# Late-converted weights used from the tiles they are converted into, in turns with loaded ones

## The chip, the core and the metric

The kernel runs on one core of a Trainium2 chip. The metric is device time in microseconds (us) of one execution; the median of three runs stands for the kernel. TensorE (PE) multiplies, VectorE (DVE), ScalarE (ACT) and GpSimd (POOL) work on elements, and SyncE (SP) asks for transfers between HBM and the on-chip buffers. In the kernel before all transfers are asked for by SP's queue, which goes through its list in order.

## What is computed

The reference chains three parts over 2304 tokens (4 batches of 576), cut here to what matters:

```python
q_p, k_p = phi(q), phi(k)                  # linear attention, 4 batches x 8 heads
x = (q_p @ (k_p.T @ v)) / (q_p @ sum(k_p)) # -> x: 2304 x 512
h = x @ w_in                               # first layer, 512 -> 2048
x = (h * cos(h)) @ w_out                   # second, 2048 -> 512
P = sinkhorn(x @ w_gate)                   # 8 experts
out = sum(P[:, e:e+1] * (relu(x @ w1[e]) @ w2[e]) for e in range(8))
```

The weights `w_in` and `w_out` arrive as 64-bit numbers, viewed as pairs of 32-bit integers.

## The kernel before

Every fp32 product is made of three products of rounded parts: a number is split into `hi` (fp32r) and `lo = x - hi`, and a product is `hi*hi + hi*lo + lo*hi`. Each weight therefore exists as a pair of tiles.

**Weights of the middle part.** `w_in` and `w_out` are cut into 16 **units** of 128 hidden columns (`NF1`). A unit has two **halves** of 512 KB: half `2f` is the piece of `w_in` of unit f (tile `wi`), half `2f+1` the piece of `w_out` (tile `wo`). So there are 32 halves, 0 to 31. A half is **converted** from its 64-bit form in seven operations, each on 128 x 512 elements:

- `conv_fetch` (L124): SP loads the raw half into `raw64`, of which there are two buffers (the profile calls the source `in_moe_w_dram`);
- `conv_low` (L129): ACT makes `csgn` from the low words;
- `conv_size` and `conv_floor` (L135, L140): DVE makes and clips `cmag`; `conv_high` (L144): DVE shifts `cmag`, and takes the sign into `csgn`;
- `conv_join` (L149): POOL adds `csgn` to `cmag`;
- `conv_round` (L153): ACT copies to the `hi` part; `conv_rest` (L158): POOL subtracts to the `lo` part. Both go into a tile `csp` of a pool of its own;
- `conv_store` (L162): SP stores `csp` to HBM as `wd[f]`. `load_half1` (L96) loads it again later, into `wi` or `wo`, of which there are four buffers each.

**Order of the work.** `attention()` runs 16 head pairs through a software pipeline whose order is the string `ORDER`; one half is converted in each turn, halves 0 to 16 in all. Then the middle part goes over five blocks of tokens: blocks 0 to 2 (512 tokens, one after the other), and blocks 3 and 4 together. For one block `moe1_steps` (L579) walks over the 16 units: `moe1_l1` makes 12 products for unit f into `ph`, the function `h*cos(h)` follows in five operations (ACT `y`, ACT `t`, DVE `y`, ACT `y` (the sine), DVE `h`) and the split of its result in two more (ACT `hh`, DVE `hl`), and `moe1_l2` of unit f, 12 products into `acc`, is issued two units later (`LAG`). Each 6 products are a **step**; a unit is four steps.

The generator `convert()` (L379) converts halves 17 to 31. Each `next(conv)` issues a third of a half's work, and in block 0 one is issued after every step:

```python
for blk in range(B - 1):
    for i, _ in enumerate(moe1_steps(blk)):
        tick()
        if blk == 0:
            next(conv, None)
```

`weights1` (L572) loads the units in the order 0 to 15, each `wi` two units ahead, and pulls more of `conv` where a half that is to be loaded isn't converted. The order of the engines' instructions is written out in this way and kept; where the loads stand in SP's queue is chosen by a scheduler. Block 0 is therefore the only block in which half of the weights are made while they are needed; blocks 1 to 4 load all of them from `wd`. The last part (the experts) follows and is not touched.

In names below, `raw_2989` is the raw half 18, and the next numbers follow half by half; `wd_97` to `wd_112` are the stored units 0 to 15.

Of the kernel before, what the change touches and what calls it, by code (L numbers as in the profile page):

```python
# [9 lines left out]
F32 = mybir.dt.float32  # L10
F32R = mybir.dt.float32r
# [14 lines left out]
def kernel(ctx: ExitStack, tc: tile.TileContext, q, k, qk_rem, v, w_phi,  # L26
                         moe_w, moe2_w_gate, moe2_w1, moe2_w2, out):
    nc = tc.nc
    P = 128
    B, NP, _, MAIN = q.shape  # L30
    D = v.shape[-1]
    NTT, _, DM = out.shape
# [3 lines left out]
    NF1 = moe_w.shape[0]  # L36
# [38 lines left out]
    pe, ve, se, ge = Engine(nc.tensor), Engine(nc.vector), Engine(nc.scalar), Engine(nc.gpsimd)  # L75
# [5 lines left out]
    def pool_lo(lo, raw, hi):  # L81
        ge.tensor_tensor(out=lo, in0=raw, in1=hi.bitcast(F32), op=ALU.subtract)
# [4 lines left out]
    def act_hi(hi, raw):  # L87
        se.copy(out=hi, in_=raw)
# [4 lines left out]
    ps_h = ctx.enter_context(tc.tile_pool(name="ps_h", bufs=1, space=PSUM))  # L93
    wpool = mctx.enter_context(tc.tile_pool(name="wpool", bufs=4, side="right"))

    def load_half1(f, i):  # L96
        w = wpool.tile([P, 2, DM], F32R, name=f"w{'io'[i]}")
        nc.sync.dma_start(out=w.bitcast(F32), in_=wd[f][:, i, :, :])
        parts = [w[:, s, :] for s in range(2)]
        return [x.rearrange("p (k f) -> p k f", k=KC) for x in parts] if i == 0 else parts  # L100

# [11 lines left out]
    vpool = ectx.enter_context(tc.tile_pool(name="vpool", bufs=2))  # L113
    apool = actx.enter_context(tc.tile_pool(name="apool", bufs=2, side="right"))
# [4 lines left out]
    wd = [dpool.tile([P, 2, 2, DM], F32, name=f"wd{f}") for f in range(NF1)]  # L119
# [4 lines left out]
    def conv_fetch(h):  # L124
        raw = vpool.tile([P, DM, 2], I32, name="raw64")
        nc.sync.dma_start(out=raw.rearrange("p f t -> p (f t)"), in_=moe_w32[h // 2, h % 2])
        halves[h] = {"raw": raw}

    def conv_low(h):  # L129
        st = halves[h]  # L130
        st["sgn"] = vpool.tile([P, DM], I32, name="csgn")
        se.activation(out=st["sgn"].bitcast(F32), in_=st["raw"][:, :, 0].bitcast(U32), func=AF.Copy,
                      scale=2.0 ** -51, bias=2.0)

    def conv_size(h):  # L135
        st = halves[h]
        st["mag"] = vpool.tile([P, DM], I32, name="cmag", bufs=3)
        ve.tensor_scalar(out=st["mag"], in0=st["raw"][:, :, 1], scalar1=2 ** 31 - 1, scalar2=None, op0=ALU.bitwise_and)
# [10 lines left out]
    def conv_join(h):  # L149
        st = halves[h]  # L150
        ge.tensor_tensor(out=st["mag"], in0=st["mag"], in1=st["sgn"], op=ALU.add)

    def conv_round(h):  # L153
        st = halves[h]
        st["sp"] = vpool.tile([P, 2, DM], F32R, name="csp")
        act_hi(st["sp"][:, 0, :], st["mag"].bitcast(F32))

    def conv_rest(h):  # L158
        st = halves[h]
        pool_lo(st["sp"][:, 1, :], st["mag"].bitcast(F32), st["sp"][:, 0, :])  # L160

    def conv_store(h):  # L162
        st = halves.pop(h)
        nc.sync.dma_start(out=wd[h // 2][:, h % 2, :, :], in_=st["sp"].bitcast(F32))

    VW = 66
    vx_t = []
# [11 lines left out]
    def load_heads(b, p):  # L179
        st = {"b": b, "p": p}  # L180
        for nm, src in (("k", k), ("q", q)):
            st[nm] = apool.tile([P, MAIN], F32, name=f"T{nm}")
            nc.sync.dma_start(out=st[nm], in_=src[b, p])
        st["r"] = apool.tile([P, P], F32, name="Tr")
        nc.sync.dma_start(out=st["r"], in_=qk_rem[b, p])
        return st
# [13 lines left out]
    first = load_heads(0, 0)  # L200
# [9 lines left out]
    def defer(n, fn):  # L210
        late.append([n, fn])
# [112 lines left out]
    def normalize(st):  # L324
        pn = st["pn"]
        pv = pn.rearrange("p (a c) -> p a c", a=2)[:, :, 0:4 * VW].rearrange("p a (j c) -> p a j c", j=4)
        pz = pn[:, 4 * VW:5 * VW]
        r = apool.tile([P, 9], F32, name="rd", bufs=2)
        rv = r[:, 0:8].rearrange("p (a j) -> p a j", a=2)
        ve.tensor_scalar(out=rv, in0=pv[:, :, :, D], scalar1=1e-6, scalar2=None, op0=ALU.add)  # L330
        ve.tensor_scalar(out=r[:, 8:9], in0=pz[:, D:D + 1], scalar1=1e-6, scalar2=None, op0=ALU.add)
        ve.reciprocal(r, r)
        xn = apool.tile([P, 4, 2, D], F32, name="xn")
        xr = apool.tile([P, D], F32, name="xr")
        ve.tensor_tensor(out=xn.rearrange("p j a d -> p a j d"), in0=pv[:, :, :, 0:D], in1=rv.unsqueeze(3).to_broadcast([P, 2, 4, D]), op=ALU.mult)
        ve.tensor_scalar(out=xr, in0=pz[:, 0:D], scalar1=r[:, 8:9], scalar2=None, op0=ALU.mult)
        st["xn"], st["xr"] = xn, xr
# [41 lines left out]
    def convert():  # L379
        first = B * NP + 1  # L380
        for h in range(first, NHALF + 2):
            if h < NHALF:
                if h not in halves:
                    conv_fetch(h)
                conv_low(h)
                conv_size(h)
                conv_floor(h, ve)
            if h - 2 >= first:
                conv_rest(h - 2)
            yield  # L390
            if h < NHALF:
                conv_high(h)
            if first <= h - 1 < NHALF:
                conv_round(h - 1)
            if h - 2 >= first:
                conv_store(h - 2)
                done_conv[0] = h - 1
            yield
            if h < NHALF:
                conv_join(h)  # L400
            if h + 1 < NHALF and h + 1 not in halves:
                conv_fetch(h + 1)
            yield

    def attention():
        n = B * NP
        sts = {0: first}
        conv_fetch(0)
        conv_fetch(1)
        for i in range(n + 2):  # L410
            cur, prev, last = sts.get(i), sts.get(i - 1), sts.pop(i - 2, None)
            if i + 1 < n:
                sts[i + 1] = load_heads(*divmod(i + 1, NP))
            shared.clear()
            for step in ORDER.split():
                if step in CONV:
                    h = i - (step in ("csp", "q"))
                    if 0 <= h <= n:
                        CONV[step](h)
                        if step == "q":  # L420
                            conv_store(h)
                        if step == "c" and h + 2 < NHALF:
                            conv_fetch(h + 2)
                    continue
                if step == "KS" and cur and not prev:
                    load_values(cur)
                if step in STEP0:
                    if cur:
                        STEP0[step](cur)
                elif step in STEP1:  # L430
                    if prev:
                        STEP1[step](prev)
                    if step == "KS" and cur:
                        load_values(cur)
                elif last:
                    STEP2[step](last)
# [125 lines left out]
        defer(1, turn_logits)  # L562

    LAG = 2
    ORDER = "PK PQ Fr X rK csp sK F rQ Z xf q d KS a xh sQ PR eQ kvz csg G rR sR eQr c zh p xl Gr eK eKr n"
    MD = 1
    GD = 3

    units = [[], []]
    NU = NF1 * B  # L570

    def weights1(i, g):  # L572
        while len(units[i]) <= min(g, NU - 1):
            n = len(units[i])
            while done_conv[0] <= 2 * n + i and n < NF1:
                next(conv)
            units[i].append(load_half1(n % NF1, i))

    def moe1_steps(*blks):  # L579
        pend = []  # L580
        for f in range(NF1 + LAG):
            if f < NF1:
                g0 = blks[0] * NF1 + f
                weights1(0, g0 + 2)
                weights1(1, g0)
                unit = units[0][g0], units[1][g0]
                gs = []
                for blk in blks:
                    g = []
                    yield from moe1_l1(blk, unit, g)  # L590
                    gs.append(g)
                pend.append((f, unit, gs))
            if f >= LAG:
                f2, unit2, gs = pend.pop(0)
                for blk, g in reversed(list(zip(blks, gs))):
                    yield from moe1_l2(blk, f2, unit2, *g)
        for blk in reversed(blks):
            defer(1 if blk == B else GD, lambda blk=blk, x2=moe1_out(blk): gate(blk, *x2))
            yield 0.2
# [4 lines left out]

    done_conv = [0]
    conv = convert()

    pinned[0] = True
# [91 lines left out]
    ahead = combine_ahead()  # L700
# [167 lines left out]
    pend = None  # L868
# [3 lines left out]
    for i, (p, e, qd) in enumerate(order):  # L872
# [19 lines left out]
        pend = (p, e, qd, w2, hs)  # L892
# [61 lines left out]
```

## Time and profile before

| | us |
|---|---|
| median of 3 runs (2126.04 to 2128.81) | 2128.31 |
| the profiled execution, its own time | 2126.54 |
| its span | 2124.8 |
| PE busy | 2080.5 (98%) |
| ACT busy | 923.8 (43%) |
| DVE busy | 1261.4 (59%) |
| POOL busy | 1128.9 (53%) |

The page cuts the span into 40 slices of 53 us. PE is busy for nine tenths or more in nearly all of them; attention fills the first three slices, block 0 stands in slices 4 to 6 (163 to 281 us), and there PE's slices read 8, 7 and 9 tenths and those of the DMA engines 7, 8 and 7, among the highest of the span. A busy share of the whole span says little here: the change works inside block 0, and that stretch has to be read by itself, with the queue of each engine. A matmul's busy time also holds the time in which its clock was low.

### The profile page before, as it was taken

Reading aid. Unit: us, or ns where it says so; the run is one execution under the profiler, and the core shown is the slowest. Engines: PE = TensorE matmul, PEld = TensorE weight load, DVE = VectorE, ACT = ScalarE, POOL = GpSimd, SP = SyncE. Lnnn points to the kernel's source line nnn. Section 1 sums busy time; section 2 is a strip of 40 time slices with the busy share of each in tenths; the row PEclk is TensorE's granted clock in tenths of the full one; section 3 lists DMA queues with packets and bytes.
Section 4 is the critical chain, followed back from the end, with each engine's and each line's share of the span. In section 5 each row is a group of like instructions: output and inputs, shape, how many; then the busy total and the mean of one; then the engine's idle time right before and its main releaser. Section 6 shows DMA issues by size and latency. Waiting matters only on the chain.

```text
span 2124.8 us, 35075 instructions
## 1 busy us (share of the span) xinstructions
PE 2080.5 (98%) x14007; PEld 1840.3 (87%) x14007; DVE 1261.4 (59%) x2281; ACT 923.8 (43%) x1436; POOL 1128.9 (53%) x760
## 2 busy tenths in 40 slices
PE   8998799999989999999999999999999999999999
PEld 7887578888878899899999999998989899999998
DVE  7886633455348756665666655555555555555555
ACT  6775544455543343334334333433343334333331
POOL 5565400000055677667666766666567666666662
PEclk9999999999999999999999999999999999999999
DMA  8857876564231122221222111611111111111101
GB/s 252 265 182 240 278 242 199 200 210 151 80 105 41 57 72 85 72 80 67 85 72 87 60 48 43 227 63 50 41 50 41 50 40 50 40 50 40 51 30 45
DMA packets 98339, 220.01 MB, mean 104 GB/s; under 512 B 31872, under 2 KB 43392, under 8 KB 98176
## 3 DMA queue, kind: packets, MB, share of 16 engines
q1 hardware_dynamic: 98176, 217.78, 31.1%
q8 instruction: 110, 1.80, 0.3%
q14 instruction: 53, 0.43, 0.1%
HBM read 183.27 MB, written 34.47 MB: 102 GB/s over the span
## 4 chain that ended last, share of the span: by engine, by line
PE 90%; DVE 4%; DMA 2%; POOL 2%; issue 1%; ACT 1%; DVEq 0%; SPq 0%; POOLq 0%
PE py L68 36%; PE pm L68 32%; PE ph L68 8%; PE acc L68 8%; PE pk L68 2%; DMA raw<-in_moe_w_dram 2%; PE pn L68 2%; PE pp L68 1%; DVE cmag L68 1%; PE pu L68 1%; POOL cmag L68 0%; PE pr L68 0%; ACT y L68 0%; POOL csp L68 0%; DVE logit L858 0%
## 5 line engine op out<-in xcount | busy, mean ns | idle before, releaser
L834 DVE SCALAR_TENSOR_TENSOR acc<-py,logit,acc 128x512 f32<-128x512 f32 x531 | 396.6, 750 | 322.0 <-PE py L68 322.0
L68 PE MATMUL pm<-xch,w1h 128*128 128x288 f32 x1792 | 531.0, 296 | 2.9 <-DVE t L856 1.3
L68 PE MATMUL pm<-xch,w1l 128*128 128x288 f32 x1792 | 530.6, 297 | 0.0
L68 PE MATMUL pm<-xcl,w1h 128*128 128x288 f32 x1792 | 523.0, 292 | 0.0
L730 POOL TENSOR_TENSOR w1l<-raw,w1h 128x256 fp32r<-128x256 f32 x126 | 97.0, 792 | 763.1 <-ACT w1h L727 763.1
L68 PE MATMUL py<-w2h,hl 128*128 128x512 f32 x1152 | 452.2, 393 | 3.7 <-POOL hl L68 3.7
L68 PE MATMUL py<-w2l,hh 128*128 128x512 f32 x1152 | 451.6, 392 | 0.0
L68 PE MATMUL py<-w2h,hh 128*128 128x512 f32 x1152 | 450.7, 391 | 0.8 <-DVE acc L834 0.8
L68 POOL TENSOR_TENSOR hl<-r,hh 128x1152 fp32r<-128x1152 f32 x128 | 344.7, 2693 | 79.0 <-ACT hh L68 73.2
L68 PEld LDWEIGHTS pm<-xcl,w1h 128*128 128x128 f32 x1792 | 341.1, 190 | 5.3 <-issue 0.4
L68 PEld LDWEIGHTS pm<-xch,w1h 128*128 128x128 f32 x1792 | 336.6, 188 | 9.6 <-DVE t L856 1.6
L68 PEld LDWEIGHTS pm<-xch,w1l 128*128 128x128 f32 x1792 | 336.2, 188 | 0.0
L808 ACT ACTIVATE r<-r 128x1152 f32<-128x1152 f32 x128 | 149.1, 1165 | 268.4 <-DVE r L788 262.1
L68 PEld LDWEIGHTS py<-w2h,hl 128*128 128x128 f32 x1152 | 216.8, 188 | 50.2 <-POOL hl L68 4.4
L68 PEld LDWEIGHTS py<-w2h,hh 128*128 128x128 f32 x1152 | 217.1, 188 | 44.9 <-DVE acc L834 2.8
L68 PEld LDWEIGHTS py<-w2l,hh 128*128 128x128 f32 x1152 | 217.0, 188 | 42.6
L784 ACT COPY keep<-pm 128x288 f32<-128x288 f32 x256 | 101.7, 398 | 344.5 <-PE pm L68 344.5
L788 DVE TENSOR_TENSOR r<-r,pm 128x288 f32<-128x288 f32 x512 | 216.0, 453 | 41.2 <-PE pm L68 40.7
L730 POOL TENSOR_TENSOR w1l<-ssum,w1h 128x1280 fp32r<-128x1280 f32 x63 | 186.7, 2963 | 2.0 <-ACT w1h L727 0.3
L788 DVE TENSOR_TENSOR r<-keep,pm 128x288 f32<-128x288 f32 x128 | 58.2, 455 | 208.5 <-PE pm L68 203.7
L68 PE MATMUL ph<-xh,wi 128*128 128x512 f32 x512 | 172.3, 398 | 7.3 <-DMA wi<-wd 6.2
L68 PE MATMUL acc<-hh,wo 128*128 128x512 f32 x512 | 170.1, 395 | 9.4 <-ACT hh L68 9.4
(147 smaller groups left out, 2834.9 us busy)
## 6 DMA issues: line engine op xcount, KB each, us to landing
raw<-in_moe_w_dram SPq DMA_DIRECT2D x160, 512.0 KB, 3.5
wi<-wd SPq DMA_DIRECT2D x64, 512.0 KB, 4.3
wo<-wd SPq DMA_DIRECT2D x64, 512.0 KB, 4.7
wd<-csp SPq DMA_DIRECT2D x32, 512.0 KB, 3.7
xcd<-xs SPq DMA_DIRECT2D x14, 576.0 KB, 5.3
out_dram<-acc SPq DMA_DIRECT2D x18, 256.0 KB, 2.2
vx<-in_v_dram SPq DMA_DIRECT2D x17, 256.0 KB, 4.6
Tk<-in_k_dram SPq DMA_DIRECT2D x16, 256.0 KB, 5.2
```

The lines of the kernel that those rows point to most:

```text
L68: ins = call(*args, **kwargs)
L730: eng.tensor_tensor(out=lo[:, sl], in0=src, in1=hi[:, sl].bitcast(F32), op=ALU.subtract)
L784: nc.scalar.copy(out=t, in_=ps[m])
L788: nc.vector.tensor_tensor(out=r[:, u, th, :], in0=r[:, u, th, :] if a is None else ps[a], in1=ps[b], op=op)
L808: nc.scalar.activation(out=rf, in_=rf, func=AF.Relu)
L834: nc.vector.scalar_tensor_tensor(out=a, in0=py, scalar=pe, in1=a, op0=ALU.mult, op1=ALU.add)
```

## The change

Of the 15 halves that are converted late (17 to 31), none is loaded again in block 0. `conv_round` and `conv_rest` write into a tile `wi` or `wo` (`half_tile`), block 0 multiplies with it, and it is stored to `wd` for the later blocks. The store is asked for in ACT's queue (`conv_store(h, se)`). Block 0 walks over the units in the order 0, 1, 8, 2, 9, 3, 10, 4, 11, 5, 12, 6, 13, 7, 14, 15 (`SEQ`), so that a unit that is loaded and one that is fresh take turns. A half's conversion is cut into four pieces in place of three, and six pieces are issued in the last turn of attention (`EARLY`). `wo` has five buffers (four before), `xn` of attention one (two before). Positions below are places in this order, 0 to 15.

```diff
-    def load_half1(f, i):
-        w = wpool.tile([P, 2, DM], F32R, name=f"w{'io'[i]}")
-        nc.sync.dma_start(out=w.bitcast(F32), in_=wd[f][:, i, :, :])
+    def half_tile(h):
+        return wpool.tile([P, 2, DM], F32R, name=f"w{'io'[h % 2]}", bufs=(4, 5)[h % 2])
...
-    def conv_round(h):
+    def conv_round(h, sp=None):
         st = halves[h]
-        st["sp"] = vpool.tile([P, 2, DM], F32R, name="csp")
+        st["sp"] = vpool.tile([P, 2, DM], F32R, name="csp") if sp is None else sp
...
-    def conv_store(h):
+    def conv_store(h, eng=nc.sync):
         st = halves.pop(h)
-        nc.sync.dma_start(out=wd[h // 2][:, h % 2, :, :], in_=st["sp"].bitcast(F32))
+        eng.dma_start(out=wd[h // 2][:, h % 2, :, :], in_=st["sp"].bitcast(F32))
...
-        xn = apool.tile([P, 4, 2, D], F32, name="xn")
+        xn = apool.tile([P, 4, 2, D], F32, name="xn", bufs=1)
...
             if h - 2 >= first:
                 conv_rest(h - 2)
+                done_conv[0] = h - 1
             yield
             if h < NHALF:
                 conv_high(h)
             if first <= h - 1 < NHALF:
-                conv_round(h - 1)
-            if h - 2 >= first:
-                conv_store(h - 2)
-                done_conv[0] = h - 1
+                fresh[h - 1] = half_tile(h - 1)
+                conv_round(h - 1, fresh[h - 1])
             yield
             if h < NHALF:
                 conv_join(h)
+            if h - 2 >= first:
+                conv_store(h - 2, se)
+            yield
             if h + 1 < NHALF and h + 1 not in halves:
                 conv_fetch(h + 1)
             yield
...
+                    if i > n and step in EARLY:
+                        next(conv)
...
+    EARLY = "csp", "q", "d", "a", "c", "p"
...
+    NEW = B * NP // 2
+    SEQ = [0, 1] + [f for i in range(NEW - 2) for f in (NEW + i, 2 + i)] + [NF1 - 2, NF1 - 1]
...
+    def weights1(i, g, ahead=False):
+        h = 2 * (SEQ[g] if g < NF1 else g % NF1) + i
+        if g < NF1 and h > B * NP:
+            while done_conv[0] <= h and not ahead:
                 next(conv)
+            return fresh.get(h)
+        if g < NU and (i, g) not in loaded:
+            loaded[i, g] = half_tile(h)
+            nc.sync.dma_start(out=loaded[i, g].bitcast(F32), in_=wd[h // 2][:, i, :, :])
+        return loaded.get((i, g))
```

ACT's queue in block 0 before, some units in. `csgn<-raw` is `conv_low`, `csp<-cmag` is `conv_round`; there are four thirds of a half per unit, so that their place among `y`, `t`, `y`, `hh` shifts from unit to unit:

```order
L68 ACTIVATE y<-ph 128x512
L68 ACTIVATE t<-y 128x512
L68 ACTIVATE y<-y 128x512
L68 CAST hh<-h 128x512
L68 ACTIVATE csgn<-raw_3159 128x512
L68 CAST csp<-cmag 128x512
L68 ACTIVATE y<-ph 128x512
L68 ACTIVATE t<-y 128x512
L68 ACTIVATE y<-y 128x512
L68 ACTIVATE csgn<-raw_3198 128x512
L68 CAST hh<-h 128x512
L68 CAST csp<-cmag 128x512
```

The same queue now, two units out of the middle of block 0; `wo<-cmag` and `wi<-cmag` are `conv_round` into the tile that is multiplied with:

```order
L68 ACTIVATE y<-ph 128x512
L68 ACTIVATE t<-y 128x512
L68 ACTIVATE y<-y 128x512
L68 CAST hh<-h 128x512
L68 ACTIVATE csgn<-raw_3224 128x512
L68 CAST wi<-cmag 128x512
L68 DMA wd_106<-wo 128x1024
L68 ACTIVATE y<-ph 128x512
L68 ACTIVATE t<-y 128x512
L68 ACTIVATE y<-y 128x512
L68 CAST hh<-h 128x512
L68 ACTIVATE csgn<-raw_3275 128x512
```

A unit now has one `csgn`, one rounding and one store, always behind `hh` and ahead of the next unit's `y`; the store of a half stands behind the rounding of the next one.

SP's queue in block 0 before, from the middle of it; L164 is the store, L126 the fetch of a raw half, L98 a load of converted weights:

```order
L164 DMA wd_108<-csp 128x1024
L126 DMA raw_3470<-in_moe_w_dram 128x1024
L98 DMA wo<-wd_105 128x1024
L98 DMA wi<-wd_108 128x1024
L164 DMA wd_109<-csp 128x1024
L126 DMA raw_3517<-in_moe_w_dram 128x1024
L164 DMA wd_109<-csp 128x1024
L98 DMA wo<-wd_106 128x1024
L126 DMA raw_3556<-in_moe_w_dram 128x1024
```

And now, where L127 is the fetch and L589 the load:

```order
L127 DMA raw_3381<-in_moe_w_dram 128x1024
L589 DMA wi<-wd_102 128x1024
L127 DMA raw_3436<-in_moe_w_dram 128x1024
L589 DMA wo<-wd_101 128x1024
L127 DMA raw_3487<-in_moe_w_dram 128x1024
L589 DMA wi<-wd_103 128x1024
L127 DMA raw_3542<-in_moe_w_dram 128x1024
L589 DMA wo<-wd_102 128x1024
```

No store of a late half stands ahead of a fetch any more; between two fetches stands one load, of a unit that was stored during attention.

## Rows read from the trace of the kernel before

**Rows 1.** Stretches: block 0, block 1, late block 0; PE, PEld, DVE, ACT, POOL, PEclk, DMA share, GB/s.

```profile
162.89:280.91 118.02, 100.13 (x385) 76.66 (x386) 69.81 (x107) 58.08 (x97) 48.14 (x36) 0.93 0.80 269
280.91:370.11 89.20, 89.20 (x402) 73.05 (x401) 35.14 (x52) 40.80 (x66) 0.00 (x0) 1.00 0.61 203
198.00:281.00 83.00, 66.89 (x254) 49.77 (x254) 50.51 (x76) 39.55 (x67) 32.73 (x23) 0.94 0.82 280
```

**Rows 2.** Chain that ended last, in block 1: start us, us, what.

```profile
293.95 2.72 PE ph L68 x12
296.67 2.72 PE acc L68 x12
```

**Rows 3.** Waits in block 0 (163 to 282): total us, times, longest us.

```profile
ACT csgn L68 <- DMA raw<-in_moe_w_dram: 19.6, 9, 5.1
...
PE acc L68 <- ACT hh L68: 9.4, 6, 2.6
...
PE ph L68 <- DMA wi<-wd: 6.2, 3, 4.6
```

**Rows 4.** Waits of SP's own queue, same stretch.

```profile
SPq L164 <- POOL csp L68: 61.3, 16, 6.1
```

**Rows 5.** Timeline of PE: start us, us, instruction, count, [idle before, releaser].

```profile
162.89 0.79 PE L68 MATMUL ph<-xh,wi 128*128 128x512 f32 x1 [1.19 <-ACT xf L68]
...
169.03 0.64 PE L68 MATMUL ph<-xh,wi 128*128 128x512 f32 x2
...
268.28 0.79 PE L68 MATMUL ph<-xh,wi 128*128 128x512 f32 x1 [4.60 <-DMA wi<-wd]
...
272.59 0.39 PE L68 MATMUL acc<-hh,wo 128*128 128x512 f32 x1
```

**Rows 6.** Timeline of ACT: the first `hh` of block 0, and a stretch without waits.

```profile
172.43 0.62 ACT L68 CAST hh<-h 128x512 fp32r<-128x512 f32 x1 [0.75 <-DVE h L68]
...
182.03 0.67 ACT L68 ACTIVATE csgn<-raw 128x512 f32<-128x512 uint32 x1
182.60 0.60 ACT L68 CAST csp<-cmag 128x512 fp32r<-128x512 f32 x1
183.11 0.59 ACT L68 ACTIVATE y<-ph 128x512 f32<-128x512 f32 x1
183.73 0.63 ACT L68 ACTIVATE t<-y 128x512 f32<-128x512 f32 x1
```

**Rows 7.** Timeline of DVE, one unit with one half converted.

```profile
249.50 0.69 DVE L68 SCALAR_TENSOR_TENSOR csgn<-raw,csgn 128x512 int32<-128x512 int32 x1
250.11 0.68 DVE L68 SCALAR_TENSOR_TENSOR y<-t,y 128x512 f32<-128x512 f32 x1
...
252.86 0.86 DVE L68 TENSOR_TENSOR hl<-h,hh 128x512 fp32r<-128x512 f32 x1 [0.68 <-ACT hh L68]
...
254.91 0.69 DVE L68 SCALAR_TENSOR_TENSOR csgn<-raw,csgn 128x512 int32<-128x512 int32 x1
255.91 1.65 DVE L68 SCALAR_TENSOR_TENSOR y<-t,y 128x512 f32<-128x512 f32 x1 [0.32 <-ACT t L68]
```

**Rows 8.** Timeline of POOL beside it.

```profile
250.34 1.61 POOL L68 TENSOR_TENSOR cmag<-cmag,csgn 128x512 int32<-128x512 int32 x1 [1.96 <-DVE csgn L68]
251.91 1.26 POOL L68 TENSOR_TENSOR csp<-cmag,csp 128x512 fp32r<-128x512 f32 x1
255.74 1.28 POOL L68 TENSOR_TENSOR cmag<-cmag,csgn 128x512 int32<-128x512 int32 x1 [2.56 <-DVE csgn L68]
```

**Rows 9.** POOL early in block 0: the first and last of four sums of an expert's weights.

```profile
168.23 1.28 POOL L719 TENSOR_TENSOR ssum<-raw 128x512 f32<-128x512 f32 x1 [3.94 <-DMA raw<-in_moe_w_dram]
...
171.32 0.73 POOL L723 TENSOR_TENSOR ssum<-raw 128x256 f32<-128x256 f32 x1
```

**Rows 10.** Tile csp, its store in SP's queue: issue ns min/median/max, first and last start.

```profile
L164 SPq DMA_DIRECT2D wd<-csp x32: 319/326/1387, 16.5 to 261.5; - x32
```

**Rows 11.** DMA issues from 140 to 290 us: count, size, median us to landing.

```profile
raw<-in_moe_w_dram SPq DMA_DIRECT2D x17, 512.0 KB, 4.7
```

More of the change, by code (lines that the diff above doesn't have):

```diff
@@ L94, with parts1 @@
     wpool = mctx.enter_context(tc.tile_pool(name="wpool", bufs=4, side="right"))
-    def load_half1(f, i):
-        w = wpool.tile([P, 2, DM], F32R, name=f"w{'io'[i]}")
-        nc.sync.dma_start(out=w.bitcast(F32), in_=wd[f][:, i, :, :])
+    def half_tile(h):
+        return wpool.tile([P, 2, DM], F32R, name=f"w{'io'[h % 2]}", bufs=(4, 5)[h % 2])
+    def parts1(w, i):
         parts = [w[:, s, :] for s in range(2)]
@@ L567 @@
     GD = 3
-    units = [[], []]
     NU = NF1 * B
[L572 to L575, printed above, removed]
-                next(conv)
-            units[i].append(load_half1(n % NF1, i))
+    NEW = B * NP // 2
+    SEQ = [0, 1] + [f for i in range(NEW - 2) for f in (NEW + i, 2 + i)] + [NF1 - 2, NF1 - 1]
+    loaded = {}
+    fresh = {}
+    def weights1(i, g, ahead=False):
+        h = 2 * (SEQ[g] if g < NF1 else g % NF1) + i
+        if g < NF1 and h > B * NP:
+            while done_conv[0] <= h and not ahead:
+                next(conv)
+            return fresh.get(h)
[3 more added lines that the diff above has]
+        return loaded.get((i, g))
     def moe1_steps(*blks):
@@ L583, in moe1_steps @@
                 g0 = blks[0] * NF1 + f
-                weights1(0, g0 + 2)
-                weights1(1, g0)
-                unit = units[0][g0], units[1][g0]
+                for j in range(0 if f == 0 else 2, 3):
+                    weights1(0, g0 + j, True)
+                wi = parts1(weights1(0, g0), 0)
+                weights1(1, g0, True)
+                unit = wi, g0
                 gs = []
@@ L591, in moe1_steps @@
                     gs.append(g)
-                pend.append((f, unit, gs))
+                pend.append((f, unit[1], gs))
             if f >= LAG:
-                f2, unit2, gs = pend.pop(0)
+                f2, g2, gs = pend.pop(0)
+                unit2 = None, parts1(weights1(1, g2), 1)
                 for blk, g in reversed(list(zip(blks, gs))):
```

## The prediction

> **What bounds the kernel now.** Only block 0 is touched, so I read the stretches first: block 0 takes 118.02 us with PE busy for 100.13 at a granted clock of 0.93, block 1 does the same products in 89.20 at 1.00 [rows 1]. Block 1's extra is its gate products; the products of one unit are 2.72 + 2.72 = 5.44 us [rows 2], 16 units 87.0 us. Block 0 thus loses 118.0 - 87.0 = 31.0 us: 17.9 in which PE stands still, and 13.1 in which it runs at the lower of its two clock levels after it stood still. That is all the change can win there.
>
> Then the waits. PE waits for `hh`, the result of ACT and DVE, and for loads of `wi` [rows 3]. ACT in turn waits 19.6 us for raw halves. Why do these come late? SP's own queue says it: 61.3 us, 16 times, SP stood in front of a store whose POOL operation wasn't done [rows 4], and in SP's order a fetch stands right behind each store. Conversion is a loop that slows itself: the late store delays the fetch, the fetch delays `csgn` on ACT, and with it the function of the unit, for which PE waits. The last wait is a chain of another kind: half 30 is stored, loaded again and then used, and PE stands for 4.60 us [rows 5].
>
> **The change, part by part.** Times below are of the profiled execution, 2126.54 us; its block 0 ends at 280.91. The order of the queues shows that the fresh tiles are read by PE and that no late store is left on SP.
>
> *Start.* ACT now has half 18's `csgn` ahead of the copies that the first product of block 0 waits for: one operation, some 0.6 us [rows 6]. PE starts at 163.5. As now, its first 14 products take 6.14 us (162.89 to 169.03 [rows 5]), 0.44 each: the lower level, 1.2 GHz, after the loose end of attention, and nothing in the change removes that. Products of positions 0 and 1 are 24, so position 2 starts at 163.5 + 6.14 + 10 x 0.227 = 171.9, and position p, if PE never waits, at 171.9 + 5.44 (p - 2): position 15 at 242.6.
>
> *Pace of conversion.* One half per unit (four pieces, four steps) where before it was one and a third. Is one half per 5.44 us possible? DVE goes in a circle: `y` starts at 250.11, `hl` at 252.86, the sign operation `csgn` at 254.91; after the sign operation the next `y` can follow 0.61 later (249.50 to 250.11). That is 2.75 + 2.05 + 0.61 = **5.41 us** [rows 7]. ACT beside it: from `csgn` to the end of `t` 183.73 + 0.63 - 182.03 = 2.33 us [rows 6], to which the change adds the asking for a store. DVE offers 2.05 + 0.61 = 2.66, so 0.3 us are free. What the asking costs ACT the trace doesn't show, since no transfer is asked for there. Bounds: nothing, as a gain has no reason; and the longest one on SP, 1.39 us; the median is 0.33 [rows 10], which I take, as it is the same request. That leaves a pace of **5.45 us**, as good as PE's 5.44. The store also waits for POOL's second operation of the half before; that ends 1.57 + 1.26 us after the start of the join [rows 8], so 0.3 us into the next unit, and the store is asked for 1.1 us into it. Behind it on ACT is the next `y`; by these rows it isn't held.
>
> *Fetches.* A raw buffer is free after the sign operation and needed two units later at `csgn`, some 10.9 - 2.7 = 8 us; landing takes 4.7 [rows 11]. SP has one load between two fetches, and it waits for a buffer that PE left a unit or more before. So the 19.6 us of ACT's waits go, with 3 us to spare. Transfers: per two units two fetches, two loads, two stores, 3.1 MB in 10.9 us, 289 GB/s, where late block 0 now moves 280 at a share of 0.82 [rows 1]. It fits, barely.
>
> The rule that speaks against the store's move: the Trainium skill, page "DMA: Bandwidth & Descriptors", section "Rules for kernel authors", says that spreading transfers over queues gives no bandwidth, only the time of issue; by it the move is worth 15 x 0.33 = 5 us of SP, which is on no path. Rows 4 say otherwise of this kernel: what it takes from SP is not bandwidth but a wait of 61.3 us with the fetches behind it.
>
> *Where the end falls.* Let L(u) be the start of `hl` at position u. The first `hh` is at 172.43 now [rows 6], so L(0) is about 173.1 + 0.6 = 173.7. Positions 0 and 1 carry half the pieces: 2.75 us from `y` to `hl`, with ACT's `y` and `t` (1.25) and once `csgn` (0.57) ahead of it, give steps of 4.65 and 4.1, L(2) = 182.4. Four sums on POOL (168.23 to 172.05 [rows 9]) now stand between conversions; I add 1 us: 183.4. L(13) = 183.4 + 11 x 5.45 = 243.4. There half 31 is joined, and half 30 done behind it: 2.05 + 0.83 (sign operation to join, 254.91 to 255.74) + 1.57 + 1.26 = 5.7 us later [rows 7, 8], at **249.1**. Position 15 needs half 30, and PE could have been there at 242.6. So one stall of about 6 us is left over (some of it taken earlier, at positions 4 to 14, where the same count gives a slack of only about 1 us). Then the products of position 15 at the low clock take 4.3 us (268.28 to 272.59, after such a stall [rows 5]) and three times 2.72 remain [rows 2]: 249.1 + 4.3 + 8.2 = **261.6**, against 280.91. Gain 19.3 us.
>
> *At nothing:* `xn` with one buffer, since its readers finish a turn of attention before it is written again; the loads moved out of attention, since PE's waits there are not for them; the load of half 16 that waits for its store at the start, since L(u) and not PE sets the end, which costs up to 1 us if that cover is gone. The later blocks read the same `wd`, stored tens of us ahead.
>
> So 2126.5 - 19.3 = 2107.2 for a run like the profiled one. That stood 1.8 us under the median of the runs; I predict the median: **2109**.
>
> **The rivals.**
>
> *VectorE loses its place.* POOL's join starts 0.83 us after the sign operation. In one row DVE's `y` is ahead of it and takes 0.68; in the other it comes 0.17 behind and takes 1.65, and ends when the join is over [rows 7, 8]. If asking for a store holds ACT for over 0.55 us, `y` comes behind the join in every unit: `y` then ends 2.88 + 1.82 = 4.70 after `hl`, and the next `hl` comes 252.86 - 250.79 = 2.07 later, a pace of 6.77. End: 183.4 + 11 x 6.77 + 5.7 + 12.5 = 276.1, a gain of 4.8: **2123.5**. For it: the margin is 0.2 us, and ACT's price is unknown. Against: the median request. The Trainium skill, page "SBUF — State Buffer", section "SBUF: two separate sides", says that VectorE and GpSimd share a pair of ports that one instruction holds to its end, whichever starts first; by that rule the 0.97 us are all or nothing, and the trace agrees with 0.68 and 1.65.
>
> *The fetches stay late,* because the transfers and not SP's queue hold them (289 GB/s is more than now). Then 19.6 us over 15 halves are 1.3 us more per unit, pace 6.75, and `y` behind the join on top: gain 0 to 5, **2126**. The page's rule above leads here. Against: the chain of SP's waits, and landing in 4.7 us now, at nearly that load.
>
> *PE alone sets the end,* if conversion is a unit ahead of my count: 163.5 + 6.14 + 370 x 0.227 = 253.6, gain 27.3, **2101**. Against: the circle of 5.41 doesn't catch up.
>
> *Slower:* ACT's queue is held. If a request in ACT's queue holds it for over 2.1 us, a unit takes 2.33 + 2.1 + 2.75 = 7.2 us or more and block 0 ends after 280.9; at 3 us it takes 8.1: 183.4 + 89.1 + 18.2 = 290.7, 9.8 us later, **2138**. For it: every request is on the path of ACT's `y`, 15 times. Against: the longest of 32 on SP was 1.39.
>
> **How the numbers follow.** Forecast 0.70; place lost 0.13; fetches late 0.07; PE alone 0.06; slower 0.04. About 0.2%, 4.3 us, is what a measurement of this kernel tells from no change. Faster by more: 0.70 + 0.06, half of 0.13, a third of 0.07: 0.85. Slower: 0.04. The same: 0.11. The forecast alone spans 2103 (no sums in the way, no low clock behind the stall) to 2115 (asking takes 0.5, a fetch late now and then); the range goes down to PE alone and up to near the lost place: 2100 to 2122.
>
> **What would show it.** Right: block 0 in about 98 us; SP's wait for POOL nearly gone there; ACT's wait for raw halves under 5 us; `hl` every 5.4 to 5.5 us; no wait for `hh`; one stall of PE of 4 to 6 us near the end, released by POOL. Wrong: `y` on DVE at 1.6 us in most units (place lost), ACT still waiting for raw halves (transfers), a gap behind each request on ACT (held), or attention changed by more than 1 us.

## The result, and the profile after

The changed kernel took 2107.99 us (median of 4 runs, 2104.99 to 2110.61), the kernel before 2128.56 beside it (4 runs, 2126.04 to 2129.2). The ratio is 0.9905, 95% interval 0.9888 to 0.9922: 20.6 us faster, where 19.3 were forecast. The profiled execution took 2109.16 us, its span is 2107.3. Against the profiled execution before (span 2124.8) that is only 17.5 us less: in this one attention ended 1.24 us later.

What is gained is gained in block 0. It begins at 164.68 and its last product ends at 263.57. The windows of the changed kernel, block 0 and its middle (columns as in [rows 1]):

```profile
164.68:263.57 98.89, 93.28 (x391) 75.34 (x392) 64.94 (x106) 55.97 (x95) 49.08 (x36) 0.97 0.78 277
198.00:246.00 48.00, 47.33 (x208) 38.53 (x206) 34.90 (x63) 30.83 (x54) 25.74 (x18) 1.00 0.78 281
```

Six products of block 1 (1.4 us) stand inside the first stretch, so block 0 itself takes 97.5 us against 118.0 in [rows 1]; above the 87.0 of its products 10.5 us are left of the 31.0 lost. In the middle PE runs at the full clock and stands for 0.67 us in 48. Before, from 198 to 281 us, it was busy for 66.89 of 83 at a granted clock of 0.94 [rows 1].

The waits of PE from 163 to 264 us, and two of SP's own, to be held against [rows 3, 4]:

```profile
PE ph L68 <- POOL wi L68: 4.9, 2, 3.9
PE ph L68 <- ACT xf L68: 1.7, 1, 1.7
PE ph L68 <- ACT wi L68: 0.6, 1, 0.6
...
SPq L127 <- DVE csgn L68: 54.9, 11, 7.4
...
SPq L165 <- POOL csp L68: 4.0, 1, 4.0
```

PE's waits for `hh` and for loads of `wi` are gone, and so are ACT's for raw halves; SP's wait for POOL falls from 61.3 us to 4.0. What SP waits for most now is a free raw buffer, and no late fetch follows from it: ACT doesn't wait for a raw half once in this stretch.

One position in the middle on ACT, DVE and POOL, beside [rows 6 to 8]:

```profile
227.22 0.62 ACT L68 CAST hh<-h 128x512 fp32r<-128x512 f32 x1 [0.75 <-DVE h L68]
227.75 0.66 ACT L68 ACTIVATE csgn<-raw 128x512 f32<-128x512 uint32 x1
228.24 0.33 ACTq L68 DMA_DIRECT2D wd<-wi  x1
228.32 0.60 ACT L68 CAST wo<-cmag 128x512 fp32r<-128x512 f32 x1
228.83 0.59 ACT L68 ACTIVATE y<-ph 128x512 f32<-128x512 f32 x1
...
227.88 0.87 DVE L68 TENSOR_TENSOR hl<-h,hh 128x512 fp32r<-128x512 f32 x1 [0.69 <-ACT hh L68]
...
230.53 0.69 DVE L68 SCALAR_TENSOR_TENSOR y<-t,y 128x512 f32<-128x512 f32 x1
...
233.29 0.88 DVE L68 TENSOR_TENSOR hl<-h,hh 128x512 fp32r<-128x512 f32 x1 [0.69 <-ACT hh L68]
...
230.76 1.61 POOL L68 TENSOR_TENSOR cmag<-cmag,csgn 128x512 int32<-128x512 int32 x1 [2.56 <-DVE csgn L68]
```

The pace is 233.29 - 227.88 = 5.41 us. DVE's `y` stands 0.23 us ahead of POOL's join and takes 0.69. The request for a store runs beside the rounding: `y` follows the rounding by 0.51 us, as it did without a request (182.60 to 183.11 [rows 6]).

The end of block 0 in the chain of waits:

```profile
248.56 1.27 POOL wi L68
249.83 0.04 issue
249.87 4.14 PE ph L68 x10
254.01 5.48 PE acc L68 x24
```

POOL ends half 30 at 249.8, PE has stood 3.9 us for it, and then needs 4.14 us for ten products that take 2.27 at the full clock. That one stall costs some 5.8 of the 10.5 us that are left.

### The profile page after: what moved, and what is told of

The parts are those of the page before. It is cut to its first block, busy times and chain, and to the rows that moved or that the text cites. A ratio compares the mean times of both kernels' runs of the same rounds, so it can differ in the third digit from the quotient of the medians.

```text
span 2107.3 us, 35032 instructions
## 1 busy us (share of the span) xinstructions
PE 2073.0 (98%) x14007; PEld 1838.9 (87%) x14007; DVE 1258.6 (60%) x2281; ACT 923.2 (44%) x1436; POOL 1129.9 (54%) x760
## 4 chain that ended last, share of the span: by engine, by line
PE 84%; DVE 4%; issue 1%; ACT 1%; POOL 1%; DMA 0%; DVEq 0%; SPq 0%; POOLq 0%
PE py L68 36%; PE pm L68 32%; PE ph L68 8%; PE acc L68 7%; DVE cmag L68 1%; DVE y L68 0%; ACT y L68 0%; DVE h L68 0%; ACT hh L68 0%; DVE csgn L68 0%; DVE logit L874 0%; DVE r L804 0%; DMA xs<-x2d 0%; DVE acc L844 0%; DVE logit L881 0%
```

## The experiments

Each median stands on 4 to 12 runs. Differences are to the median of the kernel before in the same job. That median moves by some 2 us between jobs, so two kernels of different jobs are compared by both columns.

| kernel | median us | ratio to before (95%) | us |
|---|---|---|---|
| the change | 2107.99 | 0.9905 (0.9888 to 0.9922) | -20.6 |
| change, late stores on SP | 2109.04 | 0.9901 (0.9886 to 0.9917) | -20.7 |
| before, late stores on ACT | 2130.66 | 1.0007 (0.9998 to 1.0015) | +0.9 |
| the same, store ahead of the rounding | 2123.55 | 0.9980 (0.9972 to 0.9989) | -4.6 |
| change, halves stored and loaded back | 2129.67 | 1.0004 (0.9994 to 1.0013) | +1.6 |
| the same, late fetches on ACT too | 2148.26 | 1.0084 (1.0070 to 1.0098) | +17.7 |
| change, no early piece | 2124.91 | 0.9982 (0.9973 to 0.9990) | -4.2 |
| change, three early pieces | 2116.19 | 0.9935 (0.9922 to 0.9949) | -14.4 |
| change, 64 columns more on ACT | 2108.83 | 0.9900 (0.9886 to 0.9915) | -20.9 |
| change, 3 x 256 columns more on ACT | 2120.00 | 0.9958 (0.9945 to 0.9971) | -8.1 |
| change, three pieces for a half | 2115.67 | 0.9942 (0.9929 to 0.9954) | -12.4 |
| change, swap at position 15 | 2105.24 | 0.9883 (0.9869 to 0.9896) | -24.5 |
| swap and a seventh early piece | 2103.71 | 0.9875 (0.9860 to 0.9891) | -25.4 |

**Which part carries the gain?** First the queue, put back alone:

```diff
-                conv_store(h - 2, se)
+                conv_store(h - 2)
```

> The changed kernel, with the late stores asked for by SP again and nothing else different. My theory: in the kernel before, SP held the next raw fetch behind a store that waited 6.1 us for GpSimd's rest; here the rest of half h ends .3 us after the start of the next position, so the fetch behind it goes out at once after it and has 5.4 us until the floor that reads it, while a raw half lands 4.7 us after it is asked for. So the fetch is just in time and the time is 0 to 4 us above that of the changed kernel: 2108 to 2112. Rival (who asks is worth only the asking itself): nothing changes, 2108 within half a us. Rival (the queue alone is the change): SP's waits for GpSimd come back to 40 us or more, ScalarE waits for raw halves again, and most of the 20 us is lost: 2120 to 2128.

It is the time of the change. That lies in my range, and by the difference to the kernel before also in the first rival's; the run can't tell these two apart. The wait is back and costs nothing that these runs can tell; SP's own waits of this run:

```profile
SPq L165 <- POOL wi L68: 25.6, 7, 9.0
SPq L165 <- POOL wo L68: 20.6, 8, 4.6
```

That is 46 us of waiting in front of fetches, and ACT waits for no raw half. Then the queue alone, in the kernel before:

```diff
-    def conv_store(h):
+    def conv_store(h, eng=nc.sync):
...
-                conv_store(h - 2)
+                conv_store(h - 2, se)
```

> The kernel before, with the late stores asked for by ScalarE's queue and nothing else different: the converted weights are still stored and loaded again. My theory: ScalarE's waits for raw halves (9 in the late part of block 0, 19.6 us) vanish, the conversion ends several us earlier, but each first-layer product still waits for a store and a reload behind it, some 4 and 5 us: block 0 is 12 to 18 us shorter than before, 2110 to 2116. Rival (asking from another queue saves only the time of the asking): 0 to 1 us, 2127 to 2128.5. Rival (the reload is the whole loss): up to 5 us faster, 2123 to 2128, with the first-layer products waiting for reloaded halves as long as before.

My theory fell: no gain. The waits of this run from 150 to 300 us:

```profile
ACT csp L68 <- DMA wd<-csp: 20.3, 11, 5.4
...
PE acc L68 <- ACT hh L68: 11.7, 7, 4.3
...
ACT csgn L68 <- DMA raw<-in_moe_w_dram: 2.8, 3, 1.6
```

ACT's 19.6 us for raw halves are down to 2.8, as I had said they would be, and ACT stands 20.3 us for one of the two `csp` tiles instead, until an earlier store has landed. The store stood behind the next rounding on ACT, so each went out only when the one before had landed. To take out this chain I turned the two round:

```diff
...
-            if first <= h - 1 < NHALF:
-                conv_round(h - 1)
             if h - 2 >= first:
-                conv_store(h - 2)
+                conv_store(h - 2, se)
                 done_conv[0] = h - 1
+            if first <= h - 1 < NHALF:
+                conv_round(h - 1)
```

> The kernel before with its late stores on ScalarE's queue, each now asked for ahead of the next half's high rounding and not behind it. In the run with the plain move every store went out only when the one before it had landed (11 waits of ScalarE's queue for a landing, 20.3 us, stores 5.5 to 7.2 us one behind the other), because the rounding ahead of it waited for the tile of two halves ago. Theory 1 (the old loss is SP's queue, and the plain move only put a chain of stores in its place): the chain breaks, ScalarE waits for no raw half, a position with 4/3 halves takes some 6.05 us for the 12 positions that convert and 5.4 for the other four: 94 us and some 3 for the start, block 0 ends at 262 to 265 in place of 281: 2109 to 2114. Theory 2 (the store and the load back are the loss, whoever asks): products wait for stored and reloaded halves, 2122 to 2130.

Only 4.6 us: theory 2. Waits of this run:

```profile
PE acc L68 <- ACT hh L68: 11.4, 5, 5.0
ACT csp L68 <- DMA wd<-csp: 9.0, 4, 6.3
...
ACT csp L68 <- POOL csp L68: 8.1, 4, 3.3
...
ACT csgn L68 <- DMA raw<-in_moe_w_dram: 2.6, 3, 1.7
```

ACT's waits for raw halves are down to 2.6 us here too, yet ACT waits 17.1 us for a `csp` tile, and PE for `hh` no less than in [rows 3]. The opposite test takes back the use of the tile in place (its store again ahead of the rounding) and leaves the rest of the change as it is written:

```diff
-                fresh[h - 1] = half_tile(h - 1)
-                conv_round(h - 1, fresh[h - 1])
+                conv_round(h - 1)
...
-            while done_conv[0] <= h and not ahead:
+            while done_conv[0] <= h:
                 next(conv)
-            return fresh.get(h)
```

> The changed kernel (turns, pieces, early pieces, stores on ScalarE's queue, one tile more) without its first part: late halves are rounded into a tile of their own, stored, and loaded back as before; the store is asked for ahead of the next half's rounding. Theory 1 (SP's queue and the turns make the gain, the tiles converted in place only save the loads): a reload lands some 8 us behind the rest of its half, but the loads are asked for two positions ahead: 2109 to 2113. Theory 2 (using the tile in place is what makes the gain): the last halves are stored and reloaded on the path, DMA carries 15 loads more in the stretch where its share is .8, first-layer products wait several times: 2118 to 2128.

Theory 2 again: the whole gain is gone. Waits of PE and ACT from 163 to 282 us in this run, then its transfers there (count, size, median us to landing):

```profile
PE ph L68 <- DMA wi<-wd: 15.3, 7, 5.9
...
ACT csp L68 <- POOL csp L68: 10.4, 2, 5.8
...
ACT csgn L68 <- DMA raw<-in_moe_w_dram: 0.7, 1, 0.7
```

```profile
wi<-wd SPq DMA_DIRECT2D x18, 512.0 KB, 6.1
wo<-wd SPq DMA_DIRECT2D x18, 512.0 KB, 7.2
wd<-csp ACTq DMA_DIRECT2D x15, 512.0 KB, 4.9
raw<-in_moe_w_dram SPq DMA_DIRECT2D x14, 512.0 KB, 6.6
```

The fetches are in time (0.7 us), and PE stands seven times for a loaded half: by these medians a store takes 4.9 us to land and a load 6.1, some 11 us for a fresh half. Two other things differ in this run, and what they cost is not separated. ACT waits for a `csp` tile again. And since a load is asked for two positions ahead, it pulls the conversion of its half forward, so that the pieces lose their even place: `y` on DVE takes 1.2 to 1.5 us at six of the 16 positions, where the changed kernel shows 0.69 at every one from position 3 on. One of the six:

```profile
218.96 1.45 DVE L68 SCALAR_TENSOR_TENSOR y<-t,y 128x512 f32<-128x512 f32 x1 [0.54 <-ACT t L68]
```

In the changed kernel the same view of transfers reads, over 163 to 264 us:

```profile
raw<-in_moe_w_dram SPq DMA_DIRECT2D x14, 512.0 KB, 3.7
wo<-wd SPq DMA_DIRECT2D x12, 512.0 KB, 5.0
wi<-wd SPq DMA_DIRECT2D x11, 512.0 KB, 4.7
```

There are 23 loads in 101 us in place of 36 in 119, and transfers land sooner, a raw half in 3.7 us in place of 6.6; that the fewer loads are the reason is not shown. Last, an attempt to free the fetches from SP's waits for landings:

```diff
-                conv_fetch(h + 1)
+                conv_fetch(h + 1, se)
```

> The kernel that stores and loads back its late halves in turns (2129.67 us), with the late raw fetches asked for by ScalarE's queue too, so that on SP no fetch stands behind a load that waits for a store to land (43.5 us in 11 waits from 195 us on in that run). Theory 1 (the loss is the fetch held on the queue): the conversion runs free, a reload comes some 9 us behind the rest of its half, asked for two positions ahead: 2110 to 2115. Theory 2 (the loss is the way itself, store landing 3 to 6 us and load 4 to 6 us on the path of every fresh half): TensorE still waits for the reloaded first-layer halves, 10 us or more in all at low clock: 2120 to 2128.

This run tells nothing between the two: on ACT the fetch went out later, behind the sine of the position, and ACT waited 28.8 us in 14 waits for raw halves besides PE's 23.7 for reloads. Nor did `y` keep its place: 1.5 us or more at ten positions. The run can't say how the loss divides between the held fetches and the way itself.

**The early pieces.** The prediction counted them in, but gave them no price of their own.

```diff
-    EARLY = "csp", "q", "d", "a", "c", "p"
+    EARLY = ()
```

> The changed kernel without its early pieces: the attention's last turn converts nothing of the late halves, so the same 57 pieces (14.25 halves) all lie in block 0. Theory: the attention ends up to 1 us sooner; the last half is ready 6 pieces later, that is 1.5 positions of 5.42 us, 8 us; the stall ahead of position 15 grows from 3.9 to some 10 to 12 us (parts of it at positions 13 and 14), 6 to 8 us slower in all: 2114 to 2116. Rival (the pieces only trade places, since what the attention loses block 0 gains): within 1 us, 2107 to 2109.

Twice the loss that I expected: 16.4 to 16.9 us against the change. Two positions of this run on PE, DVE and POOL:

```profile
230.72 1.26 POOL L68 TENSOR_TENSOR wi<-cmag,wi 128x512 fp32r<-128x512 f32 x1
...
232.04 0.73 PE L68 MATMUL ph<-xh,wi 128*128 128x512 f32 x2 [2.04 <-POOL wi L68]
...
235.80 1.28 POOL L68 TENSOR_TENSOR wo<-cmag,wo 128x512 fp32r<-128x512 f32 x1
...
235.96 1.68 DVE L68 SCALAR_TENSOR_TENSOR y<-t,y 128x512 f32<-128x512 f32 x1 [1.55 <-ACT t L68]
239.70 0.69 DVE L68 TENSOR_TENSOR hl<-h,hh 128x512 fp32r<-128x512 f32 x1 [0.69 <-ACT hh L68]
...
243.96 1.26 POOL L68 TENSOR_TENSOR wi<-cmag,wi 128x512 fp32r<-128x512 f32 x1
245.27 0.72 PE L68 MATMUL ph<-xh,wi 128*128 128x512 f32 x2 [2.04 <-POOL wi L68]
```

Here a fresh `wi` is ready only when PE already waits for it, and PE's products, then `y`, `hl` and the conversion of the next fresh `wi` follow in a ring of 245.27 - 232.04 = 13.23 us for two positions, 6.6 for one in place of 5.4. On the way `y` falls behind POOL's subtraction and takes 1.68. The order on the engines is fixed at one half per position, so a lag of 1.5 positions is not made up here: it is paid at every second position, not once. Half the pieces:

```diff
-    EARLY = "csp", "q", "d", "a", "c", "p"
+    EARLY = "csp", "q", "d"
```

> The changed kernel with three early pieces in place of six. With none the time was 2124.91 us, and the profile showed TensorE waiting 7 times, 13.6 us, for a half just converted, and VectorE's y at 1.68 us in every second position. Theory (a fresh half must be ready before its position begins, or a whole mode of waits sets in): three pieces are .75 position, 4 us, which is more than the waits of 2 to 3 us there; the waits go but for the last, which is some 4 us longer than the 3.9 of the changed kernel: 2111 to 2114. Rival (each piece is worth its share): half of 16.9 us, 2116 to 2117.

6 to 8 us above the change, the rival's half; the waits did not go: PE still stood six times, 11.1 us, for a fresh `wi`.

**How near is the lost place?** Two kernels add copies of a constant tile, which nothing reads, behind each late store on ACT. The smaller:

```diff
...
+                for _ in range(1):
+                    se.copy(out=pad[:, 0:64], in_=pad[:, 0:64])
```

> The changed kernel, with one copy of a constant 64-column tile on ScalarE (about .2 us) added behind each late store. My theory: ScalarE has .4 us free in each position, since its sine waits 1.17 us for VectorE's y where .76 is the least that any position shows; so the copy is hidden, the pace stays 5.42 us, y stays .69 us, and the time is that of the changed kernel within half a us: 2107.5 to 2108.5. Rival (ScalarE is as tight as VectorE): 14 positions by .2 us, 3 us slower: 2111.

Hidden: the copy takes 0.24 us, and the sine's wait for `y` shrinks from 1.17 to 1.03. The larger:

```diff
...
+                for _ in range(3):
+                    se.copy(out=pad[:, 0:256], in_=pad[:, 0:256])
```

> The changed kernel, with three copies of a constant 256-column tile on ScalarE (about 1 us together) added behind each late store. ScalarE's free time of .4 us is used up, and its first activation of a position comes .6 us later. Theory (a place is lost): VectorE's y then meets GpSimd's join or rest and takes 1.5 us or more in place of .69, the pace goes from 5.42 to about 6.8 us for 13 positions: 15 to 18 us slower, 2122 to 2126. Rival (only the time beyond the free .4 counts): .6 us in each of 13 or 14 positions, 8 us slower: 2115 to 2117. Rival (it is hidden, TensorE's 24 products of 5.44 us are the real pace): 2108 to 2109.

Some 12 us slower than the change, at a pace of 6.61. POOL and DVE in this run:

```profile
210.10 1.29 POOL L68 TENSOR_TENSOR cmag<-cmag,csgn 128x512 int32<-128x512 int32 x1 [3.64 <-DVE csgn L68]
...
210.84 1.10 DVE L68 SCALAR_TENSOR_TENSOR y<-t,y 128x512 f32<-128x512 f32 x1 [0.88 <-ACT t L68]
```

The copies took 1.18 us, not 1.0; less the 0.41 that were free (the sine's 1.17 less 0.76, the least) that makes 0.77, and would be a pace of 6.2. The rest is the place, though not with the 1.5 us for `y` that I expected: `y` begins 0.74 behind the join and ends 0.55 after the join's end. In [rows 7, 8] it began 0.17 behind and also ended 0.54 after it. In these rows what `y` loses is set by the join's end, so that a lost place gives about the same pace whether `y` comes a little behind the join or more: 6.6, against the prediction's 6.77.

**Faster conversion.** Three pieces for a half, the store and the next fetch together:

```diff
-            yield
             if h + 1 < NHALF and h + 1 not in halves:
```

> The changed kernel, with three pieces for a half in place of four (the store and the next raw fetch in one piece), so that 4/3 halves are converted in a position while it lasts. Theory: VectorE's circle with a third more of the conversion takes some 6.05 us for 11 positions and 5.44 for the rest, the last half is ready some 15 us earlier, and the stall ahead of position 15 with its low clock (6 us) goes; 11 by .6 is 6.6 us lost: between 2 us faster and 3 us slower, 2106 to 2111. Rival (y loses its place in some positions): 7 positions by 1.3 us more, 2115 to 2120.

Some 8 us slower than the change, in the rival's range: the pieces shift against the function, and now and then an operation of DVE runs beside one of POOL and takes longer. DVE in this run:

```profile
211.49 1.38 DVE L68 TENSOR_SCALAR cmag<-raw 128x512 int32<-128x512 int32 x1
...
216.69 1.77 DVE L68 SCALAR_TENSOR_TENSOR y<-t,y 128x512 f32<-128x512 f32 x1
```

In steady work these take 0.41 and 0.69. It isn't the whole of the loss: the first product of block 0 waits 4.4 us for ACT here (1.73 in the change), and ACT waits 7.5 us in all, four times, for raw halves. How the 8 us divide was not separated.

**The stall that was left.** PE can do other products while half 30 is made:

```diff
+            late2 = f == NF1 - 1 and blks[0] == 0
+            if late2:
+                f2, g2, gs = pend.pop(0)
+                unit2 = None, parts1(weights1(1, g2), 1)
+                yield from moe1_l2(0, f2, unit2, *gs[0])
...
-            if f >= LAG:
+            if f >= LAG and not late2:
```

> The changed kernel, with the second-layer products of position 13 in block 0 issued before the first-layer products of position 15, so that TensorE has work while the last half is converted. My theory: the stall of 3.9 us ahead of position 15 and the low clock behind it (10 products in 4.1 us where 2.3 is the full rate) go for the most part, since no later product waits for them: 4 to 6 us faster, 2102 to 2104. Rival (the stall only moves, to the second-layer products of position 14 or 15, since the last products can't start before the last half is converted and read): within 1 us, 2107 to 2109.

Some 3.7 us faster, a little under the 4 to 6 of my theory, than the two kernels of the same job that equal the change (2109.04 and 2108.83); its four runs, 2104.39 to 2106.31, lie below all of theirs (the lowest is 2106.35). The stall ahead of position 15 in this run, and the clock stays up behind it:

```profile
248.58 0.73 PE L68 MATMUL ph<-xh,wi 128*128 128x512 f32 x2 [1.59 <-POOL wi L68]
```

A seventh early piece takes the rest:

```diff
-    EARLY = "csp", "q", "d", "a", "c", "p"
+    EARLY = "csp", "q", "csg", "d", "a", "c", "p"
```

> The kernel with the second-layer products of position 13 ahead of the first-layer products of position 15 (2105.24 us), with one early piece more (7 in place of 6). Theory: the last half is ready a quarter of a half sooner, 1.4 us, and the stall of 1.6 us that was left ahead of position 15 nearly goes, for at most .5 us more at the end of the attention: 2104 to 2105, and in the profile no wait above .5 us for the last converted half. Rival (the piece delays the attention by its whole length on GpSimd or VectorE): 2105 to 2107.

2103.71 us, the fastest of all, though not set apart from the swap alone by its interval. Block 0 (165.00 to 259.20):

```profile
165.00:259.20 94.20, 93.64 (x406) 76.72 (x408) 67.66 (x104) 58.37 (x97) 47.16 (x35) 0.98 0.82 287
```

PE stands for 0.56 us in the whole of block 0. Some 20 products that follow block 0 (about 4.5 us) stand inside this stretch. The price is at the start, where its first product waits 4.36 us for ACT in place of 1.73.

## Why the prediction was right, and where its reasons were not

**The time and the count of steps held.** From the last products of attention (160.81 before, 162.05 after) to the end of block 0 it took 120.1 us before and 100.2 without block 1's six products: 19.9 us less, 19.3 forecast. By the profile's own times block 0 was to end at 261.6; it ended at 263.57, with 1.24 us of a later attention and 1.4 us of block 1's products in it. Start: +0.6 said, +0.55 found (2.63 us in place of 2.08). `hl` at position 2: 183.4 said, 183.17 found, in part by errors that cancel (attention later, and only 0.7 of the 1 us for POOL's sums falls before it); at position 13: 243.4 and 244.13. Pace: 5.45 and 5.42. Half 30 done: 249.1 and 249.8. Stalls: one of 6 us, some of it earlier, and 0.98, 0.6 and 3.9 us found. Low clock behind the stall: 4.3 us said, 4.14 found for ten products.

**Terms of wrong size.** Asking for a store costs ACT nothing, not 0.33 us; that was the lower bound, and it is why `y` kept its place. POOL's sums cost 2.1 us, not 1: beside them DVE's `y` of position 2 took 1.39 in place of 0.69, and DVE's work on `cmag` between positions 2 and 3 took 2.69 in place of 1.30 (6.80 from `hl` to `hl`):

```profile
179.71 1.39 DVE L68 SCALAR_TENSOR_TENSOR y<-t,y 128x512 f32<-128x512 f32 x1 [0.32 <-ACT t L68]
```

At the start eight products ran at the low clock, 3.50 us (0.44 each, as in [rows 5]), not fourteen; nothing waited for that. Two sums don't come out of the terms beside them: 2.33 and 0.33 on ACT fit DVE's 2.66, so the pace they give is 5.41 and not 5.45, and the steps of 4.65 and 4.1 are 4.57 and 4.00 by theirs. Together they move the end by 0.6 us.

**The step that failed** is the cause: "Conversion is a loop that slows itself: the late store delays the fetch". The wait in [rows 4] was real, and so was ACT's in [rows 3], but the run with the stores on SP has the one without the other, and in the two runs of the kernel before where ACT's wait is down to 2.8 and 2.6 us, the gain is nothing and 4.6 us. The rule of the Trainium skill that I set aside (page "DMA: Bandwidth & Descriptors", section "Rules for kernel authors": another queue saves the time of issue and no more) came nearer: with the tiles used in place, which queue asks made no difference that these runs can tell. What the 20.6 us rest on is the use of a tile where it was converted, without which nothing of them is left, and the six early pieces, without which some 16.5 us are lost. Against the run without the first, it takes away the 11 us of storing and loading for each fresh half, the wait for a `csp` tile, and the pieces pulled forward that cost `y` its place; how the gain divides between these three was not separated. Nor was the order of turns tested by itself. The prediction gave the way through HBM a price only at half 30 [rows 5], where it was the last wait; that elsewhere it hid behind waits for `hh` is likely by the two runs of the kernel before, but not shown.

That the time came out all the same is no proof of the cause. The sum is made of the engines' pace with no wait for a fetch or a load in it, so it holds for whatever takes those waits away; here the change had the part that did, and the six early pieces to give it a lead, which the sum used without a price.

**The rivals.** The lost place is real at about the price I gave it, but not all or nothing: `y` took 1.10 where I had only 0.68 and 1.65. A copy of 0.24 us doesn't bring it on and 1.18 us do; by the rows (an estimate) `y` has 0.41 us free and stands 0.23 ahead of the join, 0.6 in all, where I had left 0.2. Fetches stay late: not seen. PE alone: reached in the middle of block 0, and nearly from end to end with the swap and the seventh piece. ACT's queue held: not seen. I had named a change of attention by over 1 us as a sign against me, and attention did end 1.24 us later in this profile; but with the same early pieces it ended at 159.41 in the run with the swap, and at 160.67 in the one with none, so the pieces don't make that difference. This profile was behind long before them: PE's third group of `pp` products from `Tk` starts at 25.18 us in place of 22.45.

## What to carry to other kernels

A long wait on a queue shows who is late, not what a faster queue is worth (46 us of it were worth nothing here): ask what the waiter's consumer would wait for next, and test the part by itself. Where data made on the chip are stored and loaded again for their first use, try them in place. Where making and using go at one pace in a fixed order, a lag is paid in every turn; buy the lead before the loop begins, here six small pieces for 16 us.

## What the runs showed of the hardware

A request for a transfer in ACT's queue took 0.33 us and ran beside ACT's own copy, 15 times, at no cost to it. VectorE's `y`, where it started behind GpSimd's join, ended 0.54 to 0.55 us after the join, whether it had begun 0.17 or 0.74 us behind it. PE, after standing 3.9 us, ran its next ten products in 4.14 us in place of 2.27; after 1.6 us nearly none was slowed (0.73 us for the first two, then 0.39 for one and 0.62 for two, as in steady work).
